# Thresholded attention and a shrink layer on one core: k and q of later pairs turned by DMA, loaded two pairs at a time from the ScalarE queue

## The chip, the cores and the metric

The kernel runs on one core of a Trainium2 chip. The metric is device time in microseconds (us) of one execution, as the median of repeated runs. Engines are named as in the profile: PE (TensorE), PEld (its weight loads), DVE (VectorE), ACT (ScalarE), POOL (GpSimd), SP (SyncE, which here only issues DMAs). A name with q, as SPq or ACTq, is the engine's instruction sequencer.

## The reference

Eight batches of eight heads; 576 rows of 64 numbers in each of q, k and v. Attention keeps, in each row, only the scores within tau of the row's maximum. Its output becomes 4608 tokens of 512 features for two layers with h - tanh(h) between them.

```python
batch, n_heads, seq, head_dim = (8, 8, 576, 64)
scores = (1 / sqrt(64)) * q @ k^T
thresh = max(scores, -1) - tau              # tau = 0.02
scores = where(scores >= thresh, scores, -1e9)
attn   = exp(scores - max(scores, -1)); attn /= sum(attn, -1) + 1e-9
x      = (attn @ v) as (4608 tokens, 512)
h      = x @ w_in                           # 512 -> 2048
out    = (h - tanh(h)) @ w_out              # 2048 -> 512, float32
```

## The kernel before

**Pairs and tiles.** The work goes by pairs of heads: 32 pairs p, four to a batch, the first batch being pairs 0 to 3. A pair has 2 x 576 = 1152 query rows, 9 tiles of 128 rows: four of each head and a ninth that holds the last 64 rows of both. So there are 288 score tiles i, and the loop over steps s runs over them: step s issues the scores of tile s + 8 (`AHEAD`), the `kink` of tile s + 3, the softmax weights and the attention product of tiles near s, and the preparation of later pairs. The engines run one program order each and wait on one another only by semaphores.

**Preparing a pair.** `load` brings k, q and v from HBM as float32, two DMAs for each, both from SP: rows 0 to 511 of the two heads with four neighbouring rows in a partition (256 KB, runs of 1 KB), and the 64 remaining rows (32 KB, runs of 256 B). `split` on POOL multiplies by 256 and cuts a value into two float16 numbers, high and low, side by side (`hl`, 128 partitions x 9 chunks x 128). `turn` transposes the nine chunks, so that the 64 + 64 high and low parts lie in partitions and the 1152 rows in columns. [...] For k, POOL then writes a copy with high and low exchanged (`kS`), since a score is the sum of two products, q with kT and q with kS. `split_v` casts v to bfloat16 with a column of ones. The remaining rows of the two heads are interleaved in chunk 4 and are put apart on the way.

**Scores to weights.** `scores` makes a tile's 576 columns in four matmuls (512 and 64 columns, kT and kS). DVE copies it out with its row maximum (L346); once in two tiles DVE makes the shift `nb` (L358). ACT makes `z` by a steep Prelu (L373), which pushes what lies below the threshold far down. For pairs 6 and later, two tiles' z are turned by one DMA transpose from SP (`zT<-z`, L380), and ACT takes exp of the result (`pT<-zT`, L409); for the first six pairs PE turns z instead. `attend` multiplies with v, `norm` divides, `emit_x` turns the result for the layers.

**The layers.** From the second batch on, the layers of the batch before lie between the attention steps: 16 pieces h (`hidden`, L505, then tanh on ACT L518 and the subtraction on DVE L524) and 16 pieces y (`project`, L531). `PATTERN(m)` is a string by hand that says at which of some 36 steps an h or a y is issued. After the last attention step (about 437 us) the rest of the layers runs by itself.

**The order of preparation.** `plan` maps a step to preparation work. With first = 9p - 8, the step of a pair's first scores, a pair's work stands d steps ahead: loads at 17 to 12, splits at 8 to 10 and 7 to 9, the turn of k at about 6, `split_v` at 4, the turn of q at 2 (PE) or 6 to 7 (DMA). At each step the plan comes after that step's scores, kink, layers and attention, in every engine's program; so a DMA from SP stands behind the zT transposes of that step and ahead of those of the next. `raw_pool`, `hl_pool` and `qk_pool` hold two buffers for each of k, q and v (for `kS` too).

Of the kernel before, what the change touches and what calls it, by code (L numbers as in the profile page):

```python
# [9 lines left out]
F32 = mybir.dt.float32  # L10
BF16 = mybir.dt.bfloat16
FP16 = mybir.dt.float16
# [6 lines left out]
def kernel(  # L19
# [11 lines left out]
    nc = tc.nc  # L31
    P = 128
# [13 lines left out]
    HPAIR = H // 2  # L46
# [85 lines left out]


    raws = {}

    def load(p, t):
        b, h0 = p // HPAIR, 2 * (p % HPAIR)
        hs = slice(h0, h0 + 2)  # L140
        src = {"k": k, "q": q, "v": v}[t]
        eng = nc.sync
        r = raws[p, t] = raw_pool.tile([P, 10, D], F32, name=f"{t}raw", tag=t)
        n = 8 if t == "v" else 10
        eng.dma_start(
            out=r[:, 0:n, :].rearrange("p (h c) d -> p h (c d)", h=2)[:, :, 0 : 4 * D],
            in_=src[b, hs, 0:512, :].rearrange("h (p c) d -> p h (c d)", c=4),
        )
        rem = src[b, hs, 512:S, :].rearrange("h s d -> s h d")
        if t == "v":  # L150
            eng.dma_start(out=r[0:64, 8:10, :], in_=rem)
        else:
            eng.dma_start(out=r[:, 4, :], in_=rem)

    def load_first(t, h, eng):

        src = {"k": k, "q": q}[t]
        if (0, t) not in raws:
            raws[0, t] = raw_pool.tile([P, 10, D], F32, name=f"{t}raw", tag=t)
        r = raws[0, t]  # L160
        if h is None:
            rem = src[0, 0:2, 512:S, :].rearrange("h s d -> s h d")
            eng.dma_start(out=r[:, 4, :], in_=rem)
        else:
            eng.dma_start(
                out=r[:, 5 * h : 5 * h + 4, :].rearrange("p c d -> p (c d)"),
                in_=src[0, h, 0:512, :].rearrange("(p c) d -> p (c d)", c=4),
            )
# [17 lines left out]
    def split(p, t):  # L186
        x = raws.pop((p, t))[:, 0:9, :]
        hl = hl_pool.tile([P, TPP, 2, D], FP16, name=f"{t}hl", tag=t)
        nc.gpsimd.tensor_scalar(
            out=x, in0=x, scalar1=QKSC, scalar2=1.0, op0=ALU.mult, op1=ALU.mult  # L190
        )
        nc.gpsimd.tensor_copy(out=hl[:, :, 0, :], in_=x)
        nc.gpsimd.tensor_tensor(  # L193
            out=hl[:, :, 1, :], in0=x, in1=hl[:, :, 0, :], op=ALU.subtract
        )
        hls[p, t] = hl
# [21 lines left out]

    def split_v(p):
        r, vb = raws.pop((p, "v")), vbs[p % NV]  # L220
        nc.gpsimd.tensor_copy(
            out=vb[:, :, 0:4, 0:D],
            in_=r[:, 0:8, :].rearrange("p (h c) d -> p h c d", h=2),
        )
        nc.gpsimd.tensor_copy(out=vb[0:64, :, 4, 0:D], in_=r[0:64, 8:10, :])
        nc.gpsimd.tensor_copy(out=vb[64:P, :, 5, 0:D], in_=r[0:64, 8:10, :])

    mats = {}  # L230


    by_head = lambda ap: ap.rearrange("p (s h) -> p h s", h=2)
    in_heads = lambda ap: ap.rearrange("p (h s) -> p h s", h=2)

    def turn_chunk(out, c, lhsT):
        rhs = ident_f16
        if c == 4:
            out, rhs = in_heads(out), by_head(rhs)
        nc.tensor.matmul(  # L240
            out=out, lhsT=lhsT, rhs=rhs, is_transpose=True, start=True, stop=True
        )
# [4 lines left out]
        return (6, 6)[1 - p % 2]  # L247

    def q_by_dma(p):

        return p >= 2 * HPAIR and p % 4 != 0

    def turn(p, t):
        hl = hls.pop((p, t))
        if t == "q" and q_by_dma(p):
            m = mats[p, t] = qk_pool.tile([P, W], FP16, name=f"{t}T", tag=t)
            nc.sync.dma_start_transpose(
                out=m.rearrange("p (c r) -> p c r", c=TPP),
                in_=hl.rearrange("p c a d -> p (c a d)"),
            )  # L260
            return
        ps = ps_big.tile([P, W], FP16, name=f"ps_{t}", tag="big")
        for c in range(TPP):
            turn_chunk(
                ps[:, c * P : (c + 1) * P], c, hl[:, c, :, :].rearrange("p a d -> p (a d)")
            )
        m = qk_pool.tile([P, W], FP16, name=f"{t}T", tag=t)
        nc.vector.tensor_copy(out=m, in_=ps)  # L268
        mats[p, t] = m
        if t == "k":  # L270
            sw = qk_pool.tile([P, W], FP16, name="kS", tag="ks")
            for lo, hi in ((0, D), (D, 0)):
                o, i = sw[lo : lo + D, :], m[hi : hi + D, :]
                nc.gpsimd.tensor_copy(out=o, in_=i)  # L274
            mats[p, "ks"] = sw

    def turn_first(t, part):

        hl = hls[0, t[0]]
        c0, c1 = ((0, 5), (5, TPP))[part]  # L280
        pl, tag = (ps_y, "y") if t == "ks" else (ps_h, "h")
        ps = pl.tile([P, 5 * P], FP16, name=f"ps1_{t}", tag=tag)
        for c in range(c0, c1):
            o = ps[:, (c - c0) * P : (c - c0 + 1) * P]
            if t == "ks":
                for a in range(2):
                    turn_chunk(o[64 * a : 64 * a + 64, :], c, hl[:, c, 1 - a, :])
            else:
                turn_chunk(o, c, hl[:, c, :, :].rearrange("p a d -> p (a d)"))
        if part == 0:  # L290
            mats[0, t] = qk_pool.tile([P, W], FP16, name=f"{t}T", tag=t)
        dst, n = mats[0, t][:, c0 * P : c1 * P], (c1 - c0) * P
        if part == 1 or t == "q":
            nc.scalar.copy(out=dst, in_=ps[:, 0:n])
        else:
            nc.vector.tensor_copy(out=dst, in_=ps[:, 0:n])


    MAIN = (slice(0, 512), slice(640, W))
    REM = (slice(512, 576), slice(576, 640))  # L300
    scs, mxs, nbs, zs, zts, pts, ops = {}, {}, {}, {}, {}, {}, {}

    def kind(i):
# [9 lines left out]
    def scores(i):  # L313
        p, hh, t = place(i)
        qT, kT, kS = mats[p, "q"], mats[p, "k"], mats[p, "ks"]
        ps = ps_big.tile([P, 1024], F32, name="psS", tag="big")
        main, rem, lo = slice(0, 512), slice(512, 576), 0
        if kind(i) == "B":
            main, rem, lo = slice(512, 1024), slice(448, 512), 448
        if hh is None:  # L320
            qrem = REM
            if q_by_dma(p):
                qrem = (slice(512, 640, 2), slice(513, 640, 2))
            for n, kk in enumerate((kT, kS)):
                for dst, srcs in ((main, MAIN), (rem, REM)):
                    for hh in range(2):
                        nc.tensor.matmul(  # L327
                            out=ps[64 * hh : 64 * hh + 64, dst],
                            lhsT=qT[:, qrem[hh]], rhs=kk[:, srcs[hh]],
                            start=(n == 0), stop=(n == 1),  # L330
                        )
        else:
            lhs = qT[:, (5 * hh + t) * P : (5 * hh + t + 1) * P]
            for n, kk in enumerate((kT, kS)):
                for dst, src in ((main, MAIN[hh]), (rem, REM[hh])):
                    nc.tensor.matmul(  # L336
                        out=ps[:, dst], lhsT=lhs, rhs=kk[:, src],
                        start=(n == 0), stop=(n == 1),
                    )
        sc = sc_pool.tile([P, S], F32, name="sc")  # L340
        if kind(i) == "B":
            mx = mxs[i] = mxs.pop(i - 1)
        else:
            mx = mxs[i] = mx3[i // 2 % len(mx3)]
        c = int(kind(i) == "B")
        nc.vector.tensor_scalar(  # L346
            out=sc, in0=ps[:, lo : lo + S], scalar1=SC, scalar2=None,
            op0=ALU.mult, op1=ALU.max, accum_out=mx[:, c : c + 1],
        )
        scs[i] = sc  # L350
# [163 lines left out]
    def bend():  # L514
        while halves:
            m, n, ps = halves.pop(0)
            th = t_pool.tile([P, MB], F32, name="th")
            nc.scalar.activation(out=th, in_=ps, func=ACT.Tanh)  # L518
            ths.append((m, n, ps, th))

# [8 lines left out]
    def project(m, ms, part, ps, last, cols=slice(0, d_model)):  # L529
# [4 lines left out]
            )  # L534
        if part == 3:
            nc_ = cols.stop - cols.start
            yo = y_pool.tile(
                [P, nc_], F32, name="yo", tag="yo" if nc_ == d_model else f"yo{int(last)}",
                bufs=2 if nc_ == d_model else 1,
            )  # L540
            if last:
                nc.scalar.copy(out=yo, in_=ps)
            else:
# [16 lines left out]
    EARLY = lambda m: 3 if m else 3  # L560
    LAST = 1

    PATTERN = lambda m: '-h--h-hh--h-hh-h-hh-h--hh-h--hh-y-yy' if m == 0 else 'hyhyhyhyhyhyhyhyhyhyhyhyhyhyhyhy' if m == B - 2 else 'yhyhyyy-yhyhhyyhy-hhhyhh-hyhyhy-yhhy'

    FIRST = 3
    quarters = lambda m: [(m, ms, part) for ms in range(4) for part in range(4)]
# [112 lines left out]
    )  # L679

    plan = {}
    for p in range(1, NPAIR):
        first = TPP * p - AHEAD
        for d, f in PREP[3 if p == 1 else 0 :]:
            d -= p == 1 and d == 3
# [150 lines left out]
```

## Time and profile before

| What | Value |
|---|---|
| Median of 3 runs | 518.05 us (518.01 to 518.11) |
| The profiled execution's own time | 518.02 us |
| Its span, first to last instruction | 516.2 us |
| Busy: PE / ACT / DVE / POOL | 497.8 / 432.8 / 418.8 / 290.2 us |
| Granted TensorE clock | 1.00 |
| DMA packets | 208607, 86.79 MB, mean 168 GB/s |
| Packets' time on the SP queue's rings | 80.6% of 16 engines' span |
| DMA transposes | 117 of z, 18 of q |
| PE transposes of k / of q (L240) | 288 / 126, nine to a turn |

Busy time is the time in which an engine worked; issuing a DMA or waiting on a semaphore is not counted. A row of a tile gives the number of instructions, shortest, median and longest duration in ns, and when the first and the last began. A row of waits gives who waited for whom, us in total, how often, and the longest. PE's matmuls are pipelined and their ends are modelled, so what one of them takes from the path is read from the chain of work, not from its duration.

### The profile page before, as it was taken

The numbers are of one execution on the slowest core, as the hardware profiler recorded it, in microseconds if no ns is written. First come the engines' busy times: TensorE is split into PE (matmuls) and PEld (weight loads), VectorE is DVE, ScalarE is ACT, GpSimd is POOL, SyncE is SP. The second block draws the span as 40 slices with busy tenths as digits, with TensorE's granted clock in tenths as the row PEclk, the third lists the DMA queues.
The fourth block names the chain that finished last, engine by engine and source line by source line (L and its number), as shares of the span: only waits on it lengthen the run. The fifth ranks groups of instructions, "written<-read, shape, count | busy, mean of one in ns | idle before, by whom it ended". The sixth has DMA issues, their size and how long they took to land.

```text
span 516.2 us, 12626 instructions
## 1 busy us (share of the span) xinstructions
PE 497.8 (96%) x4540; PEld 285.3 (55%) x4606; DVE 418.8 (81%) x1179; ACT 432.8 (84%) x617; POOL 290.2 (56%) x390
## 2 busy tenths in 40 slices
PE   8999899889999999999999999999999999999997
PEld 4666566555555555555555555555555555544444
DVE  5999889998899988998899888998999887644440
ACT  5999999999899989998999989998999899543430
POOL 8999999776565656566666656566656620000000
PEclk9999999999999999999999999999999999999999
DMA  7852659999999999999999998999989976311013
GB/s 205 259 151 90 205 196 227 165 190 181 193 190 190 207 203 194 187 193 212 201 176 190 197 220 195 183 198 197 203 179 193 172 140 116 97 41 42 20 43 82
DMA packets 208607, 86.79 MB, mean 168 GB/s; under 512 B 176160, under 2 KB 200992, under 8 KB 208544
## 3 DMA queue, kind: packets, MB, share of 16 engines
q1 hardware_dynamic: 207952, 85.56, 80.6%
q8 instruction: 36, 0.59, 0.5%
q10 hardware_dynamic: 592, 0.43, 0.3%
q14 instruction: 27, 0.22, 0.1%
HBM read 36.70 MB, written 9.44 MB: 89 GB/s over the span
## 4 chain that ended last, share of the span: by engine, by line
PE 77%; POOL 9%; ACT 4%; DVE 3%; issue 3%; DMA 2%; SPq 1%; POOLq 0%; ACTq 0%; DVEq 0%
PE psY L531 22%; PE psH L505 19%; PE psS L336 18%; PE psO L439 5%; PE psS L327 3%; PE psHt L505 3%; PE ps_k L240 3%; POOL kS L274 2%; DMA kraw<-in_k_dram 2%; POOL w_in_sb L655 1%; PE psO L450 1%; ACT pT L409 1%; POOL khl L193 1%; PE psO L432 1%; ACT z L373 1%
## 5 line engine op out<-in xcount | busy, mean ns | idle before, releaser
L373 ACT ACTIVATE z<-sc,nb 128x576 bf16<-128x576 f32 x288 | 217.5, 770 | 23.9 <-DVE nb L358 22.2
L346 DVE TENSOR_SCALAR_CACHE_REDUCE sc<-psS 128x576 f32<-128x576 f32 x288 | 213.7, 752 | 17.5 <-PE psS L336 13.3
L531 PE MATMUL psY<-w_out_sb,g 128*128 128x512 bf16 (+1 forms) x565 | 140.2, 373 | 1.3 <-issue 0.2
L409 ACT ACTIVATE pT<-zT 128x1152 f16<-128x1152 bf16 x117 | 134.8, 1152 | 1.7 <-DMA zT<-z 1.4
L274 POOL COPY kS<-kT 64x1152 f16<-64x1152 f16 x62 | 70.7, 1141 | 110.9 <-DVE nb L358 59.6
L505 PE MATMUL psH<-xT,w_in_sb 128*128 128x512 bf16 x443 | 117.8, 379 | 3.5 <-issue 1.1
L336 PE MATMUL psS<-kT,qT 128*128 128x512 f16 (+1 forms) x512 | 104.4, 285 | 4.7 <-DVE sc L346 2.4
L336 PEld LDWEIGHTS <-qT 128*128 128x128 f16 x1024 | 72.9, 97 | 56.5 <-issue 5.5
L524 DVE SCALAR_TENSOR_TENSOR g<-th,psH 128x512 bf16<-128x512 f32 x128 | 87.5, 683 | 18.3 <-ACT th L518 18.0
L336 PE MATMUL psS<-kS,qT 128*128 128x512 f16 x496 | 101.4, 286 | 0.0
L518 ACT ACTIVATE th<-psH 128x512 f32<-128x512 f32 x128 | 74.5, 582 | 20.9 <-PE psH L505 20.9
L531 PEld LDWEIGHTS <-g 128*128 128x128 bf16 x592 | 51.1, 98 | 54.0 <-DVE g L524 0.4
L505 PEld LDWEIGHTS <-w_in_sb 128*128 128x128 bf16 x576 | 49.0, 98 | 56.3 <-issue 3.4
L439 PE MATMUL psO<-vb,pT 128*128 128x65 bf16 x1024 | 53.3, 194 | 0.0
L439 PEld LDWEIGHTS <-pT 128*128 128x128 f16 x1024 | 44.2, 98 | 9.4
L193 POOL TENSOR_TENSOR khl<-kraw,khl 128x576 f16<-128x576 f32 x31 | 39.7, 1280 | 2.6
L193 POOL TENSOR_TENSOR qhl<-qraw,qhl 128x576 f16<-128x576 f32 x31 | 39.7, 1280 | 2.6
L401 ACT ACTIVATE pT<-psZ 128x512 f16<-128x512 bf16 (+1 forms) x54 | 35.1, 654 | 2.2 <-PE psZ L392 1.8
L544 DVE COPY yo<-psY 128x512 f32<-128x512 f32 (+1 forms) x31 | 21.1, 681 | 14.7 <-PE psY L531 13.8
L465 DVE TENSOR_TENSOR osb<-psO,rc 128x256 bf16<-128x256 f32 x64 | 27.2, 424 | 2.2
L432 PE MATMUL psO<-vb,pT 128*128 128x130 bf16 x128 | 28.1, 220 | 0.1
L268 DVE COPY kT<-ps_k 128x1152 f16<-128x1152 f16 x31 | 23.4, 756 | 4.4 <-PE ps_k L240 4.3
(79 smaller groups left out, 509.7 us busy)
## 6 DMA issues: line engine op xcount, KB each, us to landing
vraw<-in_v_dram SPq DMA_DIRECT2D x32, 256.0 KB, 3.4
out_dram<-yo SPq DMA_DIRECT2D x32, 256.0 KB, 2.9
kraw<-in_k_dram SPq DMA_DIRECT2D x31, 256.0 KB, 3.3
qraw<-in_q_dram SPq DMA_DIRECT2D x31, 256.0 KB, 3.4
wt<-in_moe_w_in_dram SPq DMA_DIRECT2D x8, 512.0 KB, 4.6
wt<-in_moe_w_out_dram SPq DMA_DIRECT2D x8, 512.0 KB, 4.0
zT<-z SPq DMA_TRANSPOSE x117, 3.7
qraw<-in_q_dram SPq DMA_DIRECT2D x32, 32.0 KB, 3.1
```

What stands on the lines that cost most here:

```text
L193: nc.gpsimd.tensor_tensor(out=hl[:, :, 1, :], in0=x, in1=hl[:, :, 0, :], op=ALU.subtract)
L274: nc.gpsimd.tensor_copy(out=o, in_=i)
L336: nc.tensor.matmul(out=ps[:, dst], lhsT=lhs, rhs=kk[:, src], start=(n == 0), stop=(n == 1),)
L346: nc.vector.tensor_scalar(out=sc, in0=ps[:, lo : lo + S], scalar1=SC, scalar2=None, op0=ALU.mult, op1=ALU.max, accum_out=mx[:, c : c + 1],)
L373: nc.scalar.activation(out=z, in_=sc, func=ACT.Prelu, bias=nb, scale=1.0, alpha=STEEP)
L401: nc.scalar.activation(out=pt[:, off * P : (off + n) * P], in_=ps[:, 0 : n * P], func=ACT.Exp)
L409: nc.scalar.activation(out=pt[:, 0 : n * P], in_=zts.pop(i)[:, 0:n, :], func=ACT.Exp)
L439: nc.tensor.matmul(out=po[:, t - 1 + ab, :], lhsT=pt[:, blk * P : (blk + 1) * P], rhs=vb[:, hh, c, :], start=False, stop=(n == 7), skip_gr ...
L505: nc.tensor.matmul(out=ps, lhsT=w_in_sb[:, c, n * P : (n + 1) * P], rhs=xs[m][:, c, :] if m < B else xR[:, c, :, :], start=(c == 0), stop= ...
L518: nc.scalar.activation(out=th, in_=ps, func=ACT.Tanh)
L524: nc.vector.scalar_tensor_tensor(out=gs[m][:, n, :], in0=th, scalar=-1.0, in1=ps, op0=ALU.mult, op1=ALU.add,)
L531: nc.tensor.matmul(out=ps, lhsT=gs[m][:, n, ms * P : (ms + 1) * P], rhs=w_out_sb[:, n, cols], start=(n == 0), stop=(n == DF_C - 1),)
```

## The change

For pairs p >= 8 (`DUAL`):

- k and q of all pairs are turned by DMA transposes from SP. The exchange of high and low for `kS` becomes a step of its own (`swap`, "kw" in the plan).
- `load` is called for even p and brings two pairs: k in one DMA (rows 9r + c, nine neighbouring rows in a partition, runs of 2304 B), v in two DMAs (rows 9r + c too, 64 partitions each, runs of 1024 and 1280 B), q in three (runs of 1 KB, and 256 B for the remaining rows of each pair). They are issued from ACT's queue. The raw buffers are twice as large.
- Since k's columns come in another order, the scores read kT and kS in eight runs of 64 columns for a head (`main_keys`), in the order in which v's rows lie.
- The distances in the plan are given by `LATER`, apart for even and odd pairs; `PATTERN` has other strings for batches 1 to 5, with the same 16 h and 16 y.
- The last output halves take their buffers from the pool of `th`.

Pairs 0 to 7 keep their way.

```diff
+    DUAL = 8
     def load(p, t):
         b, h0 = p // HPAIR, 2 * (p % HPAIR)
+        src = {"k": k, "q": q, "v": v}[t]
+        eng = nc.scalar if p >= DUAL else nc.sync
+        both = raw_pool.tile([P, 2, 10, D], F32, name=f"{t}raw", tag=t)
+        if p >= DUAL:
+            raws[p, t], raws[p + 1, t] = both[:, 0, :, :], both[:, 1, :, :]
+            rows = src[b, h0 : h0 + 4, :, :]
+            if t == "v":
+                rows = rows.rearrange("h (p c) d -> p h (c d)", c=TPP)
+                dst = both.rearrange("p a (h c) d -> p (a h) (c d)", h=2)
+                eng.dma_start(out=dst[0:64, :, 0 : 4 * D], in_=rows[:, :, 0 : 4 * D])
+                eng.dma_start(out=dst[64:P, :, :], in_=rows[:, :, 4 * D :])
+            elif t == "q":
+                eng.dma_start(
+                    out=both.rearrange("p a (h c) d -> p (a h) (c d)", h=2)[:, :, 0 : 4 * D],
+                    in_=rows[:, 0:512, :].rearrange("h (p c) d -> p h (c d)", c=4),
+                )
+                for a in range(2):
+                    eng.dma_start(
+                        out=both[:, a, 4, :], in_=rows[2 * a : 2 * a + 2, 512:S, :]
+                    )
+            else:
+                eng.dma_start(
+                    out=both[:, :, 0:TPP, :].rearrange("p a c d -> p a (c d)"),
+                    in_=rows.rearrange("(a h) s d -> a (h s) d", a=2).rearrange(
+                        "a (p c) d -> p a (c d)", c=TPP
+                    ),
+                )
+            return
...
     def q_by_dma(p):
-        return p >= 2 * HPAIR and p % 4 != 0
+        return p >= DUAL
+
+    def k_by_dma(p):
+        return p >= DUAL
 
     def turn(p, t):
         hl = hls.pop((p, t))
-        if t == "q" and q_by_dma(p):
-            m = mats[p, t] = qk_pool.tile([P, W], FP16, name=f"{t}T", tag=t)
+        if (q_by_dma if t == "q" else k_by_dma)(p):
+            m = mats[p, t] = qk_tile(t)
             nc.sync.dma_start_transpose(
...
+    def swap(p):
+        m = mats[p, "k"]
+        sw = qk_tile("ks")
+        for lo, hi in ((0, D), (D, 0)):
+            o, i = sw[lo : lo + D, 0:W], m[hi : hi + D, 0:W]
+            nc.gpsimd.tensor_copy(out=o, in_=i)
+        mats[p, "ks"] = sw
...
+    def main_keys(p, kk, hh):
+        if p < DUAL:
+            return kk[:, MAIN[hh]]
+        return kk[:, 0 : 8 * P].rearrange("p (a n r) -> p n a r", a=2, n=4)[
+            :, :, :, 64 * hh : 64 * hh + 64
+        ]
+    def rem_keys(p, kk, hh):
+        return kk[:, 8 * P + 64 * hh : 8 * P + 64 * hh + 64] if p >= DUAL else kk[:, REM[hh]]
...
-    PATTERN = lambda m: '-h--h-hh--h-hh-h-hh-h--hh-h--hh-y-yy' if m == 0 else 'hyhyhyhyhyhyhyhyhyhyhyhyhyhyhyhy' if m == B - 2 else 'yhyhyyy-yhyhhyyhy-hhhyhh-hyhyhy-yhhy'
+    PATTERN = lambda m: '-h--h-hh--h-hh-h-hh-h--hh-h--hh-y-yy' if m == 0 else 'yhyhhyhh-yyhyyhhhyy-hhyyhy-hyhyy-hhy' if m == 1 else 'hyhyhyhyhyhyhyhyhyhyhyhyhyhyhyhy' if m == B - 2 else 'yhyhhyhh-yyhyyhhhyy-hhyyhy-hyhyy-hhy'
...
+    LATER = {
+        0: (
+            ("kt", 8), ("ks", 9), ("vl", 15), ("kl", 17), ("kw", 2),
+            ("ql", 12), ("qs", 9), ("qt", 7), ("vs", 4),
+        ),
+        1: (
+            ("ks", 12), ("qt", 9), ("vs", 3), ("kt", 10), ("qs", 11),
+            ("kw", 9),
+        ),
+    }
+    for p in range(DUAL, NPAIR):
+        first = TPP * p - AHEAD
+        at = lambda d, f: plan.setdefault(first - d, []).append(f)
+        for what, d in LATER[p % 2]:
+            t, w = what
+            f = {
+                "l": lambda p=p, t=t: load(p, t),
+                "s": lambda p=p, t=t: split_v(p) if t == "v" else split(p, t),
+                "t": lambda p=p, t=t: turn(p, t),
+                "w": lambda p=p, t=t: swap(p) if k_by_dma(p) else None,
+            }[w]
+            at(d, f)
+    for p in range(1, DUAL):
-    for p in range(1, NPAIR):
```

## The prediction

> **What bounds the kernel now.** I read the page first (busy times, DMA queues, costliest groups), then busy times by stretch, the chain of work that ended last in a stretch of 12 us, the waits, and the DMA list. By busy time PE stands first (497.8 us of 516.2), then ACT 432.8 and DVE 418.8. The stretches say where PE ends the steps (columns: stretch, its length, then busy us and instructions of PE, PEld, DVE, ACT, POOL, granted clock, DMA share, GB/s):
>
> ```profile
> 80.00:108.00 28.00, 25.93 (x274) 15.92 (x275) 25.55 (x75) 25.88 (x39) 23.36 (x29) 1.00 0.99 182
> 108.00:128.00 20.00, 18.64 (x172) 10.25 (x174) 17.82 (x53) 19.24 (x26) 13.79 (x19) 1.00 0.99 189
> 128.00:402.00 274.00, 270.88 (x2512) 154.46 (x2555) 246.34 (x705) 254.00 (x345) 168.72 (x215) 1.00 1.03 195
> ```
>
> From 128 to 402 us PE is idle for 3.1 us of 274; ACT is second with 92.7%. From 108 to 128 us ACT is first with 96.2%, so ACT can run at least that full. The chain inside the middle agrees:
>
> ```profile
> 245.45 0.26 PE psO L439 x8
> 245.70 0.22 PE psX L482 x4
> 245.93 0.03 PE psX L488
> 245.96 0.50 PE ps_k L240 x9
> 246.46 0.49 PE psS L336 x4
> 246.95 0.86 PE psY L531 x4
> ```
>
> It is PE alone, and one turn of k (nine 128x128 transposes, L240) stands in it with 0.50 us, less than the 0.67 us that the nine show as busy, since their ends overlap the next work. A step is one score tile; pair 9's q turn at 108.0 us and pair 31's at 413.5 us lie 198 steps apart, so a step takes 1.54 us and a pair (9 steps) about 14.0 us.
>
> **PE and DVE: what is removed.** Pairs 8 to 31 lose the PE turn of k (24) and of q where p is a multiple of 4 (8, 12, ... 28: 6). That is 30 turns of 0.50 us on the path and 30 copies L268 of 0.756 us on DVE (22.7 us, beside PE now: nothing by itself). In 128 to 402 us lie 180 and 45 of these transposes, 20 + 5 turns; with pair 31's at 413.9 us that makes 26 where PE ends the steps: 13.0 us. The other 4 (k of 8, 9, 10, q of 8) fall where ACT ends them: between 0 and 2.0 us; I take 0.5, because ACT's largest wait there is one for DVE's nb, and DVE gets lighter.
>
> **ACT, next in line.** Without the turns the middle stretch would last 274 - 25 x 0.50 = 261.5 us, in which ACT's 254.0 us are 97.1%. At the 96.2% seen above it needs 264.0 us, 2.5 us more: I take these off. (Back to back, z, pT and th start 0.67, 1.05 and 0.47 us apart, 12.6 us a pair; so ACT fits if nothing is late. Ends: 0 to 2.5.)
>
> **The loads move from SP to ACT.** Two pairs had 12 load issues on SP and now have six on ACT: one for k, two for v, three for q, at 17, 15 and 12 steps ahead; 12 double pairs make 72. The rows:
>
> ```profile
> L165 ACTq DMA_DIRECT2D qraw<-in_q_dram x2: 515/562/610, 1.4 to 2.1; - x2
> L163 ACTq DMA_DIRECT2D kraw<-in_k_dram x1: 670/670/670, 0.7 to 0.7; - x1
> L380 SPq DMA_TRANSPOSE zT<-z x117: 1242/1477/2679, 80.6 to 439.8; - x117
> ```
>
> At 0.56 us, 72 issues are 40 us of ACT's sequencer. They cost time only if ACT has nothing queued meanwhile. At the start it had nothing, and its first instruction waited 2.6 us behind three issues. In the middle I took, from the trace's instruction records, the semaphore instruction ahead of each ACTIVATE as the moment when the sequencer had got that far: it lies ahead of the next z's start by 0.94 us at least and 1.85 us in the median (174 cases). So the single issue (0.56) is covered, two (1.12) nearly always, three (1.68) in most places: a loss of 0.05 us (after a pT) or 0.19 us (after a th) for three. Ends: 0 and, if each issue must also stand behind a whole transpose on SP (0.56 + 1.48 us), 6.1 + 4.1 + 2.0 - 3 x 1.85 = 6.6 us for two pairs. No row has an issue on ACT beside a transpose on SP; the nearest rows are the issues at the start, made on both queues together in 0.37 to 0.67 us on either. So I take 1 us in all. What queues behind an ACT issue is the next z, and behind that its zT; the raw buffers that the loads write have been free for many steps, so no semaphore holds the issue.
>
> [...]
>
> **The SP queue.** A pair's loads take 0.55 + 0.57 + 0.59 + 0.56 + 0.58 + 0.65 = 3.5 us there, 4.5 zT 6.7 us, 0.75 qT of 1.34 us 1.0 us, a store 0.5 us: 11.7 of 14.0 us. After: 6.7 + 2 x 1.34 + 0.5 = 9.9 us. SP is eased. But two waits are new on it, and zT queues behind both. kT goes out 8 or 10 steps ahead of use and is wanted by POOL's swap first: landing (3.3 us, as qT) plus the swap (2 x 1.14 us) is 5.6 us of 12 to 15: covered. An even pair's q is loaded 12 steps ahead and turned 7 ahead: 5 x 1.5 = 7.5 us for three issues (1.7), landing (3.2 to 4.6, the latter a 512 KB weight piece) and POOL's split (0.67 + 0.66 + 1.28): 7.5 to 8.9 us. So SP may wait up to 1.4 us once in two pairs, with zT behind it. zT lands 2.7 us (median; 0.7 us at the tenth percentile) before pT starts, so most of this is hidden: I take 1 us in all for late zT, ends 0 and 12 x 1.4 = 17.
>
> [...]
>
> **DMA engines.** A transpose moves 1152 packets of 256 B, 0.295 MB. A pair moves 5.25 of them, 0.885 MB of loads and 0.295 MB of stores (2.73 MB; at 14.0 us that is the 195 GB/s of the row). After: 6.5, 3.10 MB.
>
> ```profile
> 241.60:243.40 1.80, 1.80 (x18) 1.02 (x16) 1.72 (x5) 1.72 (x2) 1.15 (x1) 1.00 1.25 285
> zT<-z SPq DMA_TRANSPOSE x117, 3.7
> SPq L380 <- ACT z L373: 95.7, 65, 3.1
> ```
>
> A share over 1 means that packets overlap in an engine, so it is no fill level. In a dense 1.8 us of transposes 285 GB/s flowed. At that rate 6.5 transposes take 6.7 us, and loads and stores at the 259 GB/s of the page's best slice 4.6 us: 11.3 of 13.4 us, room. If instead 195 GB/s is all there is, a pair takes 15.9 us. I take the dense row, because SP's queue waits for z, not z for the queue, and landings stay at 3.7 us.
>
> **At nothing:** the keys' order (8 runs of 64 columns as moving operand; the transposes of chunk 4, whose moving operand is strided, fit in the same 0.67 us for nine); the new order of h and y steps (the same 16 + 16); POOL's swaps (same number, and POOL is 62% busy in the middle); the tail's yo buffers.
>
> **Sum.** Against the profiled execution (518.02 us, span 516.2 and 1.8 around it; the median of the runs is 518.05): -13.0 - 0.5 + 2.5 + 1 + 1 = -9.0, so **509.0 us**. By the ends of the small terms the forecast case runs from 518 - 15 to 518 - 3: 502 to 515.
>
> **Rivals.**
> 1. ACT takes over at once: PE's relief is real, but late z and pT (ACT's waits for nb are 22.2 us today) fill ACT's 20 us of idle time in the middle. 515 to 519, chance 0.12 (0.04 faster, 0.05 no change, 0.03 slower). For it: from 80 to 128 us PE and ACT together reach no more than 93 and 94%. Against it: DVE loses 22.7 us.
> 2. **Slower: ACT's issues stand behind SP's transposes.** SP makes transposes for 9.4 of 13.4 us, so a random issue meets one 7 times in 10 and waits half of it: 0.56 + 0.7 x 0.74 = 1.1 us each. Blocks of three and two then overrun the cover of 1.85 us by 1.4 and 0.3 us: 1.8 us in two pairs, 18 us over the ten double pairs of the middle. ACT needs (254 + 18) / 0.962 = 283 us for 274: with the ends about +10, 528. It decides once ACT loses 0.962 x 274 - 254 = 9.6 us there, 1 us in two pairs. Chance 0.12, 519 to 540.
> 3. **The DMA engines become the bound.** At 195 GB/s a pair takes 15.9 us, 1.9 more, over 24 pairs +45: 563; halfway to the dense row about 530. For it: DMA share 1.03, and stretches of about 1 us every 14 us in which no packet starts. Against: above. Chance 0.14, 519 to 563.
>
> That the change does less than it says (k still turned on PE) I see no room for: the test is the pair number alone.
>
> **Chances.** The forecast case 0.62, rivals 0.12, 0.12, 0.14. A measurement here can tell about 0.2% (1.0 us) from no change. Faster by more: 0.62 + 0.04 = 0.66; within 0.2%: 0.05; slower: 0.03 + 0.12 + 0.14 = 0.29. The range for 8 in 10 takes in the forecast case, rival 1 and the lower third of rivals 2 and 3: 502 to 530; the likeliest case's own range is 502 to 515.
>
> **What would show it.** Right: L240 left with 72 transposes of k, 72 of q and 18 of the first swap (pairs 0 to 7), DMA transposes up from 135 to 165, PE still over 97% busy in the middle with steps of 1.49 us, ACT near 97%, ACTq issues near 0.6 us, zT landing under 5 us. Wrong: ACTq issues over 1.1 us and ACT idle after them (rival 2); zT landing at 6 us or more and pT waiting for it by tens of us (rival 3); PE idle on z or psO with ACT at 96% (rival 1).

## The result, and the profile after

The change made the kernel slower: 564.94 us median (557.64 to 578.32, 4 runs) against 518.06 us, a ratio of 1.0844 with a 95% interval of 1.0751 to 1.0937. The forecast was 509.0 us, range 502 to 530. Executions in a slower state are left out of the ratio, among them the profiled one, the longest with 578.32 us and a span of 576.5 us; so its waits add up to more than the median's loss. They are not its own alone: a kernel below that differs only in how q's remaining rows are read shows the same ones (ACT's z behind zT for 49.0 us, POOL behind q for 100.6 us).

The busy times by stretch (columns as shown of before):

```profile
80.00:108.00 28.00, 22.19 (x211) 12.37 (x209) 20.55 (x61) 22.43 (x33) 21.73 (x28) 0.97 1.10 202
108.00:128.00 20.00, 19.08 (x173) 10.43 (x172) 16.67 (x53) 17.61 (x24) 13.52 (x19) 0.96 0.96 187
128.00:402.00 274.00, 238.39 (x1948) 124.93 (x1947) 195.56 (x568) 215.41 (x294) 144.74 (x183) 0.92 1.10 186
```

From 128 to 402 us PE idles for 35.6 us, where it idled for 3.1 before, and its granted clock is 0.92 instead of 1.00. No engine has become the bound: ACT is busy for 79% of the stretch, DVE for 71%. The DMA engines move 186 GB/s, less than the 195 of before, although there is more to move.

The rows of the moved issues and of the z transposes (instructions, shortest, median and longest in ns, first and last start):

```profile
L154 ACTq DMA_DIRECT2D qraw<-in_q_dram x12: 370/378/415, 84.3 to 444.4; - x12
L159 ACTq DMA_DIRECT2D qraw<-in_q_dram x24: 536/555/1159, 84.8 to 449.7; - x24
L163 ACTq DMA_DIRECT2D kraw<-in_k_dram x12: 369/376/440, 76.4 to 434.4; - x12
L428 SPq DMA_TRANSPOSE zT<-z x117: 1242/1354/5999, 81.6 to 500.2; - x117
```

The 117 transposes of z now span 418.6 us where they spanned 359.2: 59.4 of the 60.3 us by which this span is longer lie there, the rest ahead of the first. An issue on ACT costs what was predicted. A z transpose has a lower median than before (1354 for 1477 ns), but a longest of 6.0 us. By the instruction records, 18 of the 108 transposes that SP issued from 128 to 400 us took over 2.5 us; before it was 2 of 104.

The chain that ended last by engine, and the waits (who waited for whom, us in total, times, longest):

```profile
PE 31%; DMA 31%; POOL 17%; ACT 11%; issue 5%; ACTq 2%; DVE 1%; SPq 0%; POOLq 0%; DVEq 0%
```

```profile
POOL qraw L216 <- DMA qraw<-in_q_dram: 111.8, 12, 14.3
...
PEld L480 <- ACT pT L457: 42.7, 17, 8.5
ACT z L421 <- DMA zT<-z: 40.9, 6, 9.2
PE psO L480 <- ACT pT L457: 35.1, 11, 8.0
DVE sc L394 <- ACT z L421: 34.5, 11, 7.8
```

PE's share of the chain is 31%, that of DMA as large. Twelve times, once for each load of two pairs, POOL waits some 9 us for q. The wait of z for zT looks odd: z does not read zT. One load burst shows what it is. The chain of waits in it (start, us, what):

```profile
268.32 11.32 DMA zT<-z
279.63 0.02 issue
279.65 0.55 ACTq L159
...
280.31 0.10 ACT z L421
```

The same burst in the timeline (start, us, engine, line, what; in brackets the idle time ahead and what ended it):

```profile
265.75 0.39 ACTq L163 DMA_DIRECT2D kraw<-in_k_dram  x1
268.43 0.65 ACTq L151 DMA_DIRECT2D vraw<-in_v_dram  x1
269.10 0.65 ACTq L152 DMA_DIRECT2D vraw<-in_v_dram  x1
...
268.32 3.41 SPq L428 DMA_TRANSPOSE zT<-z  x1
...
271.82 3.06 SPq L428 DMA_TRANSPOSE zT<-z  x1
...
275.60 3.93 SPq L428 DMA_TRANSPOSE zT<-z  x1
...
273.17 0.56 ACTq L159 DMA_DIRECT2D qraw<-in_q_dram  x1
...
279.65 0.55 ACTq L159 DMA_DIRECT2D qraw<-in_q_dram  x1
280.31 0.77 ACT L421 ACTIVATE z<-sc,nb 128x576 bf16<-128x576 f32 x1 [5.95 <-DMA zT<-z]
...
286.01 0.67 POOL L216 TENSOR_SCALAR qraw<-qraw 128x576 f32<-128x576 f32 x1 [11.37 <-DMA qraw<-in_q_dram]
...
277.83 1.04 PE L553 MATMUL psH<-xT,w_in_sb 128*128 128x512 bf16 x4
282.19 0.23 PE L480 MATMUL psO<-vb,pT 128*128 128x130 bf16 x1 [3.32 <-ACT pT L457]
...
284.72 1.86 PE L553 MATMUL psH<-xT,w_in_sb 128*128 128x512 bf16 x4 [1.56 <-DVE g L572]
```

Within 8 us 1.7 MB is asked for (the page's 576 KB of k, 256 and 320 of v, 512 and 32 of q). Meanwhile and after it three z transposes, one after the other, take 3.41, 3.06 and 3.93 us of SP's sequencer, where one took 1.48. The third issue for q stands on ACT for 5.9 us after the second: in the instruction records it waits for the completion semaphore that the z transpose of 268.32 also uses (the records name eight such semaphores, each for 8 to 11 of ACT's DMAs and for 32 to 35 of SP's), and that transpose lands only at 279.6. With it ACT stands, then DVE and PE. The even pair's q is there 13.3 us after its first issue, at 286.0; the prediction had 4.9 to 6.3 us (1.7 for the three issues, 3.2 to 4.6 for the landing). The held third issue has no part in this: it brings the odd pair's remaining rows, and by the records POOL waits here for the first two issues alone. After the idle time four matmuls of h take 1.86 us instead of 1.04.

Over 128 to 400 us, by the instruction and semaphore records, a z transpose starts 0.8 us after its z (mean; before 1.0), but lands 6.0 us after its start (mean; before 4.0). So the delay lies in the transpose's issue and landing, not in the wait for SP's queue.

### The profile page after: what moved, and what is told of

It reads as the page before. It is cut to its first block, busy times and chain, and to the rows that moved or that the text cites. A ratio compares the mean times of both kernels' runs of the same rounds, so it can differ in the third digit from the quotient of the medians.

```text
span 576.5 us, 12106 instructions
## 1 busy us (share of the span) xinstructions
PE 513.2 (89%) x4336; PEld 277.8 (48%) x4336; DVE 402.7 (70%) x1149; ACT 433.4 (75%) x617; POOL 291.5 (51%) x390
## 4 chain that ended last, share of the span: by engine, by line
PE 31%; DMA 31%; POOL 17%; ACT 11%; issue 5%; ACTq 2%; DVE 1%; SPq 0%; POOLq 0%; DVEq 0%
DMA zT<-z 15%; PE psY L579 11%; PE psH L553 8%; DMA qraw<-in_q_dram 7%; PE psS L384 6%; POOL kS L313 5%; DMA qT<-qhl 5%; ACT pT L457 4%; ACT z L421 4%; DMA kT<-khl 3%; PE psHt L553 2%; POOL khl L220 2%; ACT th L566 2%; PE psO L487 2%; POOL qraw L216 2%
## 5 line engine op out<-in xcount | busy, mean ns | idle before, releaser
L421 ACT ACTIVATE z<-sc,nb 128x576 bf16<-128x576 f32 x288 | 217.5, 769 | 77.4 <-DMA zT<-z 40.9
L579 PE MATMUL psY<-w_out_sb,g 128*128 128x512 bf16 (+1 forms) x592 | 150.5, 383 | 0.0
L553 PE MATMUL psH<-xT,w_in_sb 128*128 128x512 bf16 x480 | 132.6, 401 | 7.9 <-DVE g L572 7.7
L384 PE MATMUL psS<-kS,qT 128*128 128x512 f16 (+1 forms) x512 | 108.3, 294 | 4.4 <-POOL kS L313 4.4
L384 PE MATMUL psS<-kT,qT 128*128 128x512 f16 (+1 forms) x512 | 109.0, 296 | 2.7 <-DVE sc L394 1.5
L384 PEld LDWEIGHTS <-qT 128*128 128x128 f16 x1024 | 75.8, 100 | 68.6 <-issue 18.1
L553 PEld LDWEIGHTS <-w_in_sb 128*128 128x128 bf16 x576 | 50.7, 100 | 67.3 <-issue 18.8
L216 POOL TENSOR_SCALAR qraw<-qraw 128x576 f32<-128x576 f32 x31 | 20.8, 671 | 112.9 <-DMA qraw<-in_q_dram 111.8
L480 PE MATMUL psO<-vb,pT 128*128 128x130 bf16 x128 | 28.8, 225 | 35.2 <-ACT pT L457 35.1
L487 PE MATMUL psO<-vb,pT 128*128 128x65 bf16 x1024 | 55.2, 197 | 0.0
L487 PEld LDWEIGHTS <-pT 128*128 128x128 f16 x1024 | 46.0, 100 | 9.1 <-issue 0.9
L220 POOL TENSOR_TENSOR khl<-kraw,khl 128x576 f16<-128x576 f32 x31 | 39.7, 1280 | 2.6
L480 PEld LDWEIGHTS <-pT 128*128 128x128 f16 x128 | 12.8, 100 | 52.4 <-ACT pT L457 42.7
```

What stands on the lines that cost most here:

```text
L220: nc.gpsimd.tensor_tensor(out=hl[:, :, 1, :], in0=x, in1=hl[:, :, 0, :], op=ALU.subtract)
L384: nc.tensor.matmul(out=ps[:, dst], lhsT=lhs, rhs=cols(p, kk, hh), start=(n == 0), stop=(n == 1),)
L421: nc.scalar.activation(out=z, in_=sc, func=ACT.Prelu, bias=nb, scale=1.0, alpha=STEEP)
L480: nc.tensor.matmul(out=po[:, t - 1 : t + 1, :], lhsT=pt[:, 4 * P : 5 * P], rhs=vb[:, hh, 4:6, :], start=True, stop=False, skip_group_check ...
L487: nc.tensor.matmul(out=po[:, t - 1 + ab, :], lhsT=pt[:, blk * P : (blk + 1) * P], rhs=vb[:, hh, c, :], start=False, stop=(n == 7), skip_gr ...
L553: nc.tensor.matmul(out=ps, lhsT=w_in_sb[:, c, n * P : (n + 1) * P], rhs=xs[m][:, c, :] if m < B else xR[:, c, :, :], start=(c == 0), stop= ...
```

## The experiments

Each ratio is against the kernel before on the same chip. First the two halves of the change apart.

**Loads only.** PE turns as before, all else as in the change:

```diff
 def q_by_dma(p):
-    return p >= DUAL
+    return p >= DUAL and p % 4 != 0
 def k_by_dma(p):
-    return p >= DUAL
+    return False
```

> The changed kernel with PE turning all of k again and q where p is a multiple of 4, as before the change: the loads alone (two pairs in one, from ACT). T: with the old number of transposes the DMA engines carry it, 515 to 522. Q and R: the loss stays for the most part, 540 or more.

554.77 us, 1.0684 (1.0647 to 1.0720). The loads alone cost 36.7 us. The signs are those of the whole change, in its waits and in the row of its z transposes:

```profile
POOL qraw L216 <- DMA qraw<-in_q_dram: 108.7, 12, 11.0
...
ACT z L421 <- DMA zT<-z: 22.4, 6, 5.1
```

```profile
L428 SPq DMA_TRANSPOSE zT<-z x117: 1242/1307/4722, 82.0 to 482.9; - x117
```

**Turns only.** k and q of pairs 8 and later by DMA, the plan and the order of h and y as in the change; loads of single pairs from SP as before. A second run issued these loads four steps earlier (k 21 and 20 steps ahead instead of 17 and 16, and so on).

> The changed kernel's transposes of k and q by DMA, its plan and its pattern, but the loads of before: one pair at a time, from SP, rows 4r + c, remaining rows of 16 engines. Q and R: 503 to 512, what the prediction summed for the turns alone. T: 550 or more, with zT landing at 6 us or more.

> e4_turns_only with the loads four steps earlier (k 21 and 20, q 19 and 18, v 17 and 16 steps ahead), because in e4 POOL waited 102.8 us for k and kS came late. If e4's loss was POOL's order (split of the next k ahead of the exchange for this one, both behind a late load): 520 or less and POOL's wait for k under 20. T: still 535 or more, as the number of transposes is the same.

550.45 us, 1.0625 (1.0600 to 1.0650), and 550.30 us, 1.0617 (1.0598 to 1.0635). So this half too costs 32 us when it is alone, and not because the loads came too late: with earlier loads the time is the same. In the first of them POOL waited for k, and PE for POOL's exchange:

```profile
POOL kraw L216 <- DMA kraw<-in_k_dram: 102.8, 21, 9.3
...
PE psS L386 <- POOL kS L313: 34.3, 12, 4.0
```

By the instruction records SP was issuing for 91% and 93% of 128 to 400 us. In the kernel before it was 89% already; the prediction had 11.7 of 14.0 us, 84%.

**Is it SP's queue or the DMA engines?** The kernel before, with a DMA transpose added to each of the 30 turns that the change converts (in fact PE still turns, and nobody reads the copy); then the same with loads from ACT; and the kernel before with nothing but loads from ACT.

```diff
 def turn(p, t):
     ...
+        if p >= 2 * HPAIR:
+            spare = qk_pool.tile([P, W], FP16, name="spare", tag="spare")
+            nc.sync.dma_start_transpose(out=spare..., in_=hl...)
 def load(p, t):
-        eng = nc.sync
+        eng = nc.scalar if p >= 2 * HPAIR else nc.sync   # second and third run
```

> The kernel before with 30 spare DMA transposes: wherever PE turns k or q of pairs 8 to 31, SP also issues the same transpose into a buffer that nobody reads. All that waits as before, PE's work as before. T (the DMA engines or SP's queue cannot carry 165 transposes beside the loads): 530 to 545, zT late, pT waiting for it. If the loss comes from the plan's new waits (Q, R or the order on POOL), the spare transposes cost little: 518 to 522.

> e5_spare_turns (30 spare transposes beside the work of before, 548 us) with the loads of pairs 8 to 31 issued from ACT, as in e6. S (SP's sequencer is what is full: it issued for 93% of the middle in e5, 89% before): without 3.5 us of load issues a pair, SP has room, 518 to 524. D (the 16 DMA engines are full, at some 200 GB/s): the same bytes have to move, 540 or more.

> The kernel before with one word different: the loads of pairs 8 to 31 (one pair at a time, six DMAs) are issued from ACT. Q: the second queue alone costs, 530 or more, with ACT idle behind load issues and zT landing late. If only the shapes of the loads (two pairs in one, 64 partitions, two engines) or the plan cost: 517 to 522, ACT covering its issues as the prediction said.

| Run | us | Ratio (95%) | SP issuing, 128 to 400 us |
|---|---|---|---|
| Spare transposes, loads from SP | 548.14 | 1.0569 (1.0544 to 1.0594) | 93% |
| Spare transposes, loads from ACT | 520.55 | 1.0049 (1.0023 to 1.0075) | 80% |
| Loads from ACT alone | 518.66 | 1.0011 (1.0002 to 1.0021) | 60% |

The wait for zT and the stretch from 128 to 400 us, first of the run with loads from SP:

```profile
ACT pT L415 <- DMA zT<-z: 42.7, 22, 3.4
```

```profile
128.00:400.00 272.00, 253.08 (x2286) 140.42 (x2285) 220.34 (x631) 227.51 (x310) 152.39 (x194) 0.99 1.06 201
```

and then with loads from ACT:

```profile
ACT pT L415 <- DMA zT<-z: 4.1, 5, 1.3
```

```profile
128.00:400.00 272.00, 268.94 (x2496) 153.34 (x2537) 244.39 (x700) 253.52 (x344) 167.59 (x214) 1.00 1.14 221
```

The same transfers, and 27.6 us between them. The time from a z transpose's issue to its landing (the last number, us) does not make the difference; it is even shorter in the slower run, whose row stands first:

```profile
zT<-z SPq DMA_TRANSPOSE x117, 3.6
zT<-z SPq DMA_TRANSPOSE x117, 4.4
```

The lateness arises ahead of the issue: by the records a z transpose starts 3.0 us after its z in the first run and 0.03 us in the second (medians, 128 to 400 us; 0.9 in the kernel before). So what was full was SP's sequencer, and the DMA engines had room (221 GB/s). Loads on ACT cost 0.6 us. Taking the loads' issues off SP is worth 27.6 us here: with them and transposes of 1.3 to 1.5 us each (medians) it was issuing for 93% of 128 to 400 us, without them for 80%.

**Both good halves together.** DMA turns, loads of single pairs from ACT, four steps earlier.

```diff
-            ("ql", 12), ("vl", 15), ("kl", 17)                    # even pairs, two at a time
+            ("ql", 19), ("vl", 17), ("kl", 21)                    # even pairs
+            ("ql", 18), ("vl", 16), ("kl", 20)                    # odd pairs
```

> e7_turns_early (turns of k and q by DMA, loads of one pair, four steps earlier; 550 us from SP) with these loads issued from ACT. S: SP has room, and PE's relief of 15 us shows: 503 to 515, faster than before. D: 540 or more, as in e7.

513.45 us, 0.9898 (0.9874 to 0.9923): faster than both kernels, by 4.6 us against the one before. From here the question was only what is wrong with loading two pairs at once.

**Loads of two pairs from SP.** The change with `eng = nc.sync`, and the same with q 19 steps ahead instead of 12.

> The changed kernel with one word different: the loads of pairs 8 to 31 are issued from SP again. Three theories. Q (two queues): the loads hurt because they come from a second queue, where they run among the transposes and where ACT's sequencer stands behind a wait for a transpose (third q issue up to 8 us after the second). Then 505 to 520 us, no ACT wait at a load, zT landing under 6 us. R (remaining rows of q on two engines): each of the 24 small DMAs keeps all transposes behind it waiting on either queue; then still 540 or more. T (too many transposes for the DMA engines): then still 550 or more, whichever queue loads.

> e1_loads_sp with q of two pairs loaded 19 steps ahead in place of 12, because in e1 POOL waited 77.7 us for q, with the exchange for kS behind it. If the late q makes e1's loss of 21 us: 520 or less. T: 530 or more, with SP's transposes late though q is there in time.

539.27 us, 1.0399 (1.0369 to 1.0429), and 550.56 us, 1.0649 (1.0601 to 1.0696). From SP the large loads cost 25.7 us less than from ACT: nothing holds ACT there, and the granted clock in 128 to 400 us is 1.00. But SP issues for 93% of the time, and 19 of its 120 transposes from 128 to 400 us take over 2.5 us, though ACT issues no load there at all: these long issues go with the large loads, not with a second queue. The 505 to 520 us of theory Q were not reached. Loading q earlier made it worse, so q's lateness is not the cause by itself.

**The shapes.** (1) The remaining rows of q in the old order, since the change's DMAs for them are narrow: by the records of the changed kernel each gives 3 completion updates, where all its other DMAs give 16, and no more than four of the 256 B packets of two such DMAs are in flight at once, where a 32 KB load at the start, also of 128 such packets, has up to 14 (the expectations speak of two engines); (2) q in one DMA by rows 9r + c, as k (the order of the queries is not restored); (3) v in one such DMA as well.

> The changed kernel, but the 64 remaining rows of two heads of q are read row by row with the heads inside (64 x 2 x 64 in place of 2 x 64 x 64), so that the DMA can be spread over 16 engines; the interleaved columns of q are then picked with a step of two. R: most of the loss goes, 520 us or less, and POOL's wait for q (111.8 us) falls under 30. Q: some of POOL's wait goes, but ACT still waits at the third issue; 540 to 560. T: 555 or more.

> The changed kernel (565 us), but q of two pairs is loaded in one DMA by rows 9r + c, as k is, in place of three (the order of the queries is left unrestored). It takes away the small DMAs that use two engines and the second and third issue on ACT, behind which z stood for up to 8 us. If these make the loss: 525 or less and ACT's wait at loads gone. If v's loads into 64 partitions or the number of transposes make it: 545 or more.

> e12_q_like_k with v loaded in one DMA as k is, too (into all 128 partitions, the order of v's rows left unrestored): three load issues for two pairs, all with runs of 2304 B. If only the shapes of the loads cost: 503 to 515. If D: 540 or more. Between e12 and this one lies the price of v's two DMAs into 64 partitions each, whose packets of 1280 B ran beside transposes at 50 to 90 GB/s.

574.30 us, 1.1080 (1.1011 to 1.1150); 548.96 us, 1.0587 (1.0566 to 1.0609); 555.23 us, 1.0728 (1.0682 to 1.0774). The first is slower than the change, so the narrow shape of these DMAs is not the cause. With three plain DMAs of 576 KB, two pairs at a time still cost 37 us.

**Spread or bunched.** The change's own loads at 23 (k), 17 (q) and 11 (v) steps ahead instead of 17, 12 and 15; the three plain DMAs spread alike (rows of q and v in another order); and the fastest run bunched: single-pair loads, both pairs' issued in the same steps, with four raw buffers of one pair.

> The changed kernel with its three loads of two pairs spread evenly over the two pairs' steps: k 23 steps ahead, q 17, v 11 (before 17, 12, 15), all else as in the change, from ScalarE's queue. Theory 'bunching': what costs is that 1.77 MB is asked for within about five steps, so that the landings of zT wait for some 14 us in every two pairs; spread out the kernel is at 525 us or below, and the waits of pT for zT are short. Rival 'size or shape': a load of two pairs in one (576 KB) or its pieces hold the transposes up wherever it is put; the kernel stays at 545 us or above.

> Like the run in which q and v are loaded as k is, in one DMA of 2304-byte runs each (the rows of q and v are then in another order than the reference's), with the loads at 23, 17 and 11 steps ahead. Theory 'bunching': 505 to 520 us. Rival 'a single load of 576 KB is too large whenever it comes': 545 us or above. If this is at 520 or below and the kernel with the change's own pieces, spread alike, is at 545 or above, the pieces cost.

> The run with DMA turns and single-pair loads from ScalarE's queue (513.5 us), with raw tiles of one pair in four buffers and the loads of both pairs of two issued in the same steps: k 17, v 15 and q 12 steps ahead of the even pair (26, 24 and 21 ahead of the odd one). Theory 'bunching': the burst alone, with the old small loads, costs about what the loads of two pairs cost: 540 us or above. Rival 'size or shape of a load of two pairs': about 513 us, as with loads spread over the pairs.

538.66 us, 1.0386 (1.0353 to 1.0419); 522.06 us, 1.0085 (1.0055 to 1.0115); 559.67 us, 1.0820 (1.0761 to 1.0879). Spreading takes 26 us from the change and 33 us from its plain form; bunching adds 46 us to the fastest run. Against the fastest run the change loses 51.5 us and its plain form 41.8, so when the loads come decides half of the one and most of the other. (The spread runs also load k and q six and five steps earlier and v four later; a q that is merely earlier was tried from SP alone, where it lost.) The bunched kernels do not all lose in the same place. In the one with single loads, the waits show ACT held at its own issues, 12 within 12 us, with z and then PE behind them:

```profile
PEld L386 <- issue: 27.7, 19, 5.0
PE psS L386 <- DVE sc L396: 22.6, 12, 4.7
...
ACT z L423 <- issue: 19.8, 13, 5.2
ACT z L423 <- POOL khl L220: 18.5, 5, 4.6
```

and SP has only one transpose of 115 over 2.5 us. Part of this is the wait of the change's third q issue again, though the view names POOL or nothing for it. The table counts, from the instruction records, ACT loads that stood for over 1 us (since the start of ACT's instruction before, or the end of its issue before) until their completion semaphore, which a transpose from SP had used last, was free:

| Run | Such stands on ACT | us in all |
|---|---|---|
| The change | 11 | 50.4 |
| The change's loads alone | 10 | 35.2 |
| q like k, bunched | 8 | 21.4 |
| Three plain DMAs, bunched | none | 0 |
| Single loads, bunched | 11 | 31.4 |
| Two pairs spread, the change's pieces or plain | none | 0 |
| Single loads of the fastest run (513.45 us) | none | 0 |
| Single loads, evenly spread (512.50 us) | 5 | 7.4 |

So a burst costs in two ways. It holds ACT at an issue until SP's transpose has landed (5.9 us in the burst shown), and it makes that landing late (11.3 us after the start there, 4.0 in the mean of before); the three plain DMAs bunched lose 37 us without the first, with 30 of SP's 113 transposes over 2.5 us.

In the kernels with two pairs in a load such long issues of SP stay, spread or not: 23 of 121 for the change's pieces, 23 of 126 for plain ones. For the change's spread loads the wait for zT is still

```profile
ACT pT L457 <- DMA zT<-z: 33.4, 29, 3.3
```

So the expectation of 525 us or below for them failed, and the plain form missed its 520 by 2 us. Loads of two pairs hold SP's issues also when spread, and the change's pieces cost 16.6 us more than plain ones there. Part of the 26 us is the clock: from 128 to 400 us it is 1.00 in that run's profile and 0.92 in that of the bunched one, its longest execution.

**The change's order of keys for one pair at a time, and the fastest run varied.** k of a pair in one DMA and v in two, by rows 9r + c, loads 21, 18 and 15 steps ahead of every pair; the old pieces with that spacing; and the fastest run with k of odd pairs turned by PE.

> The change's order of keys (rows 9r+c, k in one DMA, v in two DMAs on 64 partitions each) with loads of one pair, spread evenly at 21, 18 and 15 steps ahead; q as before. From ScalarE's queue: five issues a pair in place of six. Theory 'bunching alone': the order and its pieces cost nothing, so 508 to 514 us, as the evenly spread run with the old pieces. Rival 'the pieces of v on 64 partitions cost also when spread' (the change's loads spread stayed at 538.7 us): 525 us or above.

> The fastest run (DMA turns, loads of one pair from ScalarE's queue, 513.5 us) with its loads spread evenly: k, q, v 21, 18 and 15 steps ahead of every pair, so one tensor's two loads each third step (before, gaps of 2, 2, 6, 2, 2 and 4 steps). Theory 'bunching': there is little bunching left to take away; 509 to 514 us, with shorter waits of pT for zT. Rival 'ScalarE is the bound there' (259 of 272 us busy): 512 to 515 us, no change.

> The fastest run (513.5 us) with k of the odd pairs from 9 on turned by PE again, as before the change, so 12 fewer DMA transposes, and 12 more PE turns of 0.50 us and DVE copies. Theory 'in that kernel PE is the bound again': +6 us, 519 us. Rival 'there the landings of zT and ScalarE are the bound': 511 to 514 us, with SP's queue and the transposes eased.

515.90 us, 0.9941 (0.9912 to 0.9970); 512.50 us (509.28 to 516.32), 0.9901 (0.9872 to 0.9931); 513.11 us, 0.9906 (0.9884 to 0.9928). The first lies between the two ranges expected for it. With one pair to a load the order 9r + c costs at most a few us (the intervals overlap). Its long issues of SP are 12 of 130, those of the old pieces with the same spacing 3 of 132: they go with the size of a load, though the shapes differ too. Spreading the fastest run further changes nothing that these runs can tell. Giving 12 turns back to PE does not cost the 6 us expected of a kernel that PE alone bounds; what the eased SP queue gave back for it was not measured apart.

The evenly spread run shows what the change could have been. Its stretch as shown of before, cut at 390 us where its attention steps end, and its chain:

```profile
128.00:390.00 262.00, 259.41 (x2309) 140.95 (x2307) 227.46 (x674) 250.36 (x343) 170.07 (x219) 1.00 1.17 231
```

```profile
PE 70%; POOL 12%; DMA 6%; ACT 4%; DVE 4%; issue 3%; ACTq 1%; SPq 0%; POOLq 0%; DVEq 0%
```

PE is busy for 99.0%, ACT for 95.6%, with 231 GB/s.

## Why the prediction was wrong

The medians of the main kernels side by side:

| | Single pairs, SP | Single pairs, ACT | Two pairs, SP | Two pairs, ACT | Two pairs, ACT, spread |
|---|---|---|---|---|---|
| Turns as before | 518.06 | 518.66 | not run | 554.77 | not run |
| All turns by DMA | 550.45 | 513.45, spread 512.50 | 539.27 | 564.94 | 538.66 |

- **PE's turns, 13.5 us, and ACT's limit, 2.5 us back:** the sign was right; the size, 11.0 us between them, is not shown. PE's relief shows once the loads are out of the way: the best kernels gain 4.6 and 5.6 us, and against the run with spare transposes (520.55), which moves the same transposes from the same queues while PE still turns, 513.45 is 7.1 us less, with another plan. PE and ACT are then as full as forecast: the evenly spread run's profiled execution took 509.28 us, with PE at 99.0% and ACT at 95.6% (forecast: over 97%, and 96.2%). But that execution, at the very forecast, is the shortest of eight that scatter by 7 us.
- **The issues on ACT, 1 us: the first step that failed.** The price of an issue was right (0.38 to 0.66 us in the medians of its lines; 0.6 us in all for the single loads). What failed is "no semaphore holds the issue": it looked at the raw buffers only. The third q issue waits for a completion semaphore shared with SP's transposes, 5.9 us in the burst shown, and z, DVE and PE wait with it; such stands sum to 50.4 us in the profiled execution. Rival 2 had the right victim with the wrong place and size. The longer issues that it reckons with, 1.1 us each in the mean, do not show in the changed kernel: with those medians, none on ACT took over 1.16 us, and the wait ahead of one was several times that. Nor do loads on ACT explain the long issues of SP, which come without them too (19 of 120 with the loads of two pairs from SP).
- **The SP queue:** "SP is eased" was right for the change (78% issuing from 128 to 400 us), but the fill of before was mis-sized: 84% by the median of a transpose, 89% by the records. So the sum could not see that 30 transposes more on SP cost 30 us if the loads stay there, and that with them the move to ACT is worth more than all of PE's relief.
- **The DMA engines and the late zT: the second step that failed.** "11.3 of 13.4 us, room", "landings stay at 3.7 us" and "I take 1 us in all for late zT, ends 0 and 17" average the loads over a pair. They come in 8 us out of 28, as DMAs of up to 576 KB. In the 14 us after the start of the burst shown z transposes take up to 3.9 us to issue (6.0 at most in the execution) and 11.3 us to land, and q takes 13.3 us where the step had 4.9 to 6.3. Measured as loads alone, this step and the one on ACT's issues cost 36.7 us together, where the sum had 1 and 1. Three plain DMAs, bunched, hold no issue on ACT and cost 37 us with all turns by DMA, so a loss of this size needs no held issue.
- **Rival 3** gave 563 us, close to the 564.94 measured, but by luck: its ceiling of 195 GB/s does not exist, since the spread run moves 231 GB/s. Of its signs the late zT came, but the wait for it showed at z (40.9 us), through the held load issue, more than at pT (4.3 us).
- **The narrow DMAs for q's remaining rows:** with the order of before the kernel was not faster (574.30 us), so this is no part of the loss.

Open is why the engines move only 179 GB/s within a burst (275 to 288 us), why an issue of SP takes up to 3.9 us there, with large loads in flight, and how the loss of a bunched kernel divides between ACT's held issues, the issues themselves and late landings; no run takes these apart. A wait of ACT's third issue on a semaphore of its own was not tried.

## What to carry to other kernels

Ask of every added transfer not only whether the average fits, but what else is asked for in the same ten microseconds, and which latency-critical DMA stands behind it. Few large loads need not be better than many small ones when a short transfer on the critical path runs beside them: here loads of one pair spread over the steps beat the change's loads of two, spread as well, by 26 us. Count what each DMA queue's sequencer issues from the records, with the mean and not the median, before adding to it: here SP stood at 89% before the change, and with 30 transposes more, moving the loads away was worth 27.6 us, more than PE's relief.

## What was not expected of the hardware

**The clock after an idle PE.** In the changed kernel the granted clock falls to one half for 3.4, 6.8 or 10.2 us, ten times, about once for each burst of loads. Busy times of two neighbouring stretches in the burst shown:

```profile
264.00:275.00 11.00, 11.00 (x98) 6.05 (x95) 9.93 (x31) 9.89 (x14) 6.95 (x9) 1.00 1.11 197
275.00:288.00 13.00, 8.12 (x59) 3.57 (x58) 5.62 (x16) 7.70 (x11) 1.84 (x3) 0.84 1.26 179
```

The mean of 0.92 over 274 us is a loss of up to 22 us of PE time in that execution. In the runs of 539.27 us (loads of two pairs from SP) and of 538.66 and 522.06 us (spread) the longest wait of PE or its weight loads is 2.5 us (here 8.5), and the clock is 1.00 from 128 to 400 us. Each of the ten falls follows idle time: in the 3.4 us ahead of it, the length of the shortest fall, PE stood idle for 1.9 to 3.4 us by the records. In the burst shown four matmuls of h then take 1.86 us instead of 1.04. So the idle time cost again after it had ended. The times of the runs go along with it: over the whole span the clock is 0.947 in the longest execution and 0.972 in the shortest.

**One set of completion semaphores for two queues.** By the records of the changed kernel the same eight semaphores serve the DMAs of both queues, and each of ACT's 74 DMAs whose semaphore another had used before began after that one had landed, 0.02 us after it at the earliest. 11 loads stood over 1 us for a transpose on SP that had nothing to do with them, 7.7 us at the longest: z stood 40.9 us in six waits behind such loads here, 22.4 us with the loads alone. Where the loads come spread, such stands of over 1 us are none or, with the loads of 512.50 us, 7.4 us in all.
